# A linear-attention and SwiGLU block: the K feature map by two activations, a transpose moved ahead, and the bursts for M hooked later

## Chip, core and metric

The kernel runs on one NeuronCore of one Trainium2 chip. The metric is device time in microseconds: the median of 6 runs before the change is 715.32 us. The profile is of one further execution, which took 715.18 us.

## What is computed

A layer norm of x (2048 rows of 1024) feeds two branches: linear attention with 32 heads of 32, and a SwiGLU network with 3584 hidden columns.

```python
qkv = (xn @ wqkv)                      # split into q, k, v, 32 heads of 32
phi = lambda t: where(t > 0, t + 1, exp(t)) + 1e-6
pq, pk = phi(q), phi(k)
kv = einsum("bhsd,bhse->bhde", pk, v)
z = einsum("bhsd->bhd", pk)
num = einsum("bhqd,bhde->bhqe", pq, kv)
den = einsum("bhqd,bhd->bhq", pq, z)[..., None] + 1e-6
s = (num / den) @ wo
g = silu((silu(xn @ w_gate) * (xn @ w_up)) @ w_down)
return x + s * g
```

The kernel writes phi as max(t, 0) + (min(exp(t), 1) + 1e-6), which is the same function.

## The kernel before

**Stages.** The 2048 rows are 16 tiles of 128. In the first stage (to about 118 us) every tile is normalised, transposed and multiplied by W_k and W_v, and the products of pk and v are summed over all tiles in three PSUM banks (`a_tile`, L892). Then come two passes of 1024 rows each, in which Q, gate, up, the attention output and the down projection are computed, with the weights loaded for each pass.

**Matrix products with seven steps.** Most products are taken two blocks by two with seven multiplications in place of eight, from sums and differences of blocks that VectorE makes (`combos` for x and W, `x_sums`, `sums` for weights). A `Set` (L580) holds the steps 1 to 7 of one product in PSUM banks: step 1's result is copied to a second bank (`put1`, a ScalarE Identity that reads ps and writes ps), step 5's to SBUF (`put5`), steps 6 and 7 have a VectorE add. A `Joint` (L649) makes step 1 or 5 of two products at once with half-width matmuls (256 columns). The first two tiles are done plainly, by `p_piece` (L879): eight matmuls of 512 columns, four for each half of the depth.

**The start.** x tiles and W_k, W_v blocks of 512 KB come in one after the other on the DMA queue of SyncE (SP). Tiles 0 and 1 are transposed on TensorE (`t_tile`, L802), eight transposes each, whose results ScalarE and VectorE copy to SBUF; the later tiles are transposed by DMA. The source names the pieces in lines 957 to 974: both pieces of tile 0 for K, then tile 1's transposes, then tile 1's pieces.

**The K and Q feature map** (`phi_evac`, L844) takes three instructions for a tile of 128 by 512: a ScalarE Exp out of PSUM (or out of SBUF, for step 7, whose sum VectorE has put there), a VectorE minimum with 1 and addition of 1e-6 (L850, SBUF to SBUF, f16), and a VectorE instruction that takes the maximum of the PSUM tile with 0 and adds (L851). K uses it 32 times, Q 32 times. The Exp results, and those of L850, have rings of two buffers each (L518, L520).

**The bursts for M.** KV, the normalised sum of pk and v, is transposed (`kvt`) and multiplied by W_o into a matrix M (`m_build`, L1053). A burst is 16 matmuls of 32 by 32 with 512 columns; it needs four free PSUM banks at once, ScalarE copies them to SBUF, and four DMAs of SP store them to `m_scratch`, from where they come back as weights about two weight pairs later. There are four bursts. Lines 1708 and 1709 hook them in pass 0: one after step 6 of each of the two Sets of gate pair 0, and the same for up pair 0.

**Who sets the order.** The code only lists the operations with what they read and write. A planner (`Plan`, L35) then places them: it holds a cost for each operation, a due time from TensorE's work (`dl`), a window of six TensorE operations in which the order may be changed (`WINDOW`), and a lead of 12 us for DMA. For ScalarE it holds the function table that is loaded and adds 1.28 us (`TABLE`) for a switch (L228). `tune` (L127) looks for holes on TensorE in its own plan and shifts operations of the other engines. Each engine then runs its list in order, with semaphore waits. So an edit of one cost or one hook can change the order of many instructions. The instructions of all operations are recorded at helper lines: matmuls at L309, transposes at L316, activations at L441, VectorE's tensor-tensor operations at L452, DMAs at L455.

Of the kernel before, what the change touches and what calls it, by code (L numbers as in the profile page):

```python
# [9 lines left out]
ACT = mybir.ActivationFunctionType  # L10
ALU = mybir.AluOpType
F32 = mybir.dt.float32
BF16 = mybir.dt.bfloat16
FP16 = mybir.dt.float16
KB = 1024
# [4 lines left out]
TABLE, DMA_SLACK, HOLD, YIELD = 1.28, 2.0, 0.1, 10  # L20
# [14 lines left out]
class Plan:  # L35
# [143 lines left out]
    def place(self, limit=1e9):  # L179
        ops = self.ops  # L180
        idle = work = 0.0
        for o in ops:
            o.npred = len(o.preds) + len(o.after)
            o.ready = 0.0
        free = {e: 0.0 for e in self.ENGS}
        dma_free = 0.0
        tab = None
        avail = {e: [] for e in self.ENGS}
        pe_next = deque(o for o in ops if o.eng == "pe")
        for o in ops:  # L190
            if o.npred == 0:
                avail[o.eng].append(o)
        order = []
        done = set()
        total = len(ops)
        while len(order) < total:
            best = None
            for e in self.ENGS:
                a = avail[e]
                if not a:  # L200
                    continue
                t = free[e]
                if e == "pe":
                    lim = None
                    n = 0
                    for o in pe_next:
                        if n >= self.window:
                            lim = o.idx
                            break
                        n += 1  # L210
                    cand = [o for o in a if lim is None or o.idx < lim]
                    if not cand:
                        continue
                    rdy = [o for o in cand if o.ready <= t + 0.05]
                    o = min(rdy, key=lambda o: o.idx) if rdy else min(cand, key=lambda o: (o.ready, o.idx))
                else:
                    rdy = [o for o in a if o.ready <= t]
                    soon = [o for o in a if o.ready > t]
                    while rdy:
                        o = min(rdy, key=lambda o: (o.dl - o.boost, o.idx))  # L220
                        q = [q for q in soon if q.ready + HOLD < t + o.busy and q.dl - q.boost + YIELD < o.dl - o.boost] if e != "sp" else ()
                        if not q:
                            break
                        rdy.remove(o)
                    if not rdy:
                        o = min(soon or a, key=lambda o: (o.ready, o.dl))
                s = max(t, o.ready)
                if e == "act" and o.tab is not None and o.tab != tab:  # L228
                    s += TABLE
                if best is None or s < best[0]:  # L230
                    best = (s, e, o)
            s, e, o = best
            if o.tab is not None:
                tab = o.tab
            o.start = s
            was = free[e]
            if o.sem is not None:
                free[e] = s + o.busy
                b = max(s + 1.8, dma_free)
                dma_free = b + o.nbytes / 340e3  # L240
                o.done = dma_free + DMA_SLACK
            else:
                free[e] = s + o.busy
                o.done = s + o.busy + o.lat
            avail[e].remove(o)
            if e == "pe":
                idle += s - was
                work += o.busy
                if work > limit:
                    return idle  # L250
                done.add(o)
                while pe_next and pe_next[0] in done:
                    pe_next.popleft()
            order.append(o)
            for q in o.succs:
                q.npred -= 1
                q.ready = max(q.ready, s + o.busy if q.eng == o.eng and (o.eng == "pe" or o in q.after) else o.done)
                if q.npred == 0:
                    avail[q.eng].append(q)
        self.order = order  # L260
        return idle
# [58 lines left out]
def build_kernel(nc, A_x, A_wqkv, A_wo, B_w_gate, B_w_up, B_w_down, out, WINDOW=6, NWARM=15, NPE=2, LEAD=12.0):  # L320
# [12 lines left out]
    with ExitStack() as es:  # L333
# [27 lines left out]
        TM = Arena("TM", 26 * KB)  # L361
# [66 lines left out]
        def pe_mm(reads, writes, mms):  # L428
            return PL.op("pe", reads, writes, partial(_mm_group, mms), mm_cost(mms))
# [10 lines left out]
        def act(reads, writes, o, i, func, src="ps", **kw):  # L440
            q = PL.op("act", reads, writes, lambda h: h.activation(o, i, func, **kw),  # L441
                      nel(o) / (1000.0 if "bias" in kw or not isinstance(kw.get("scale", 1.0), float) else 1200.0)
                      + (0.055 if src == "ps" else 0.095))
            if func != ACT.Identity:
                PL.table(q, func)
            return q

        def dve(reads, writes, fn, n, rate=0.96):
            return PL.op("dve", reads, writes, fn, n / (rate * 1000.0) + 0.07)

        def tt(reads, writes, o, a, b, op, fast=False):
            return dve(reads, writes, lambda h: h.tensor_tensor(o, a, b, op), nel(o), 1.92 if fast else 0.96)  # L452
# [65 lines left out]
        e_ring = Ring(TM, 20 * KB, 1 * KB, 2)  # L518
        q_ring = Ring(TM, 22 * KB, 1 * KB, 2)
        B_ring = Ring(TM, 24 * KB, 1 * KB, 2)  # L520
        rr_ring = Ring(TM, 20 * KB, 2 * KB, 1)
        x_ring = Ring(W, 32 * KB, 2 * KB, 4)
        xn_ring = Ring(W, 40 * KB, 2 * KB, 2)
# [48 lines left out]
        for n in range(NWARM):  # L572
            b = n % 8
# [267 lines left out]
            return ar.at(j * 8 * KB + k * 4 * KB, 4 * KB, FP16).rearrange("p (q t) -> p q t", t=512)[  # L841
                :, :, m * 128:(m + 1) * 128]

        def phi_evac(src, src_r, out_ap, out_r, kind="ps"):  # L844
            e = e_ring.take()
            ea = e.ap(FP16)
            act([src_r], [e.r], ea, src, ACT.Exp, kind)
            b = B_ring.take()
            ba = b.ap(FP16)
            dve([e.r], [b.r], lambda h: h.tensor_scalar(ba, ea, 1.0, EPS_PHI, ALU.min, ALU.add), 512, 2.6)  # L850
            dve([src_r, b.r], [out_r], lambda h: h.scalar_tensor_tensor(  # L851
                out_ap, src, 0.0, ba, ALU.max, ALU.add), 512)

        kvb = [balloc_part() for _ in range(3)]

# [10 lines left out]
        def k_evac(i, j, ap, r, kind):  # L866
            if i not in pkv:
                pkv[i] = pk_ring.take()
            s = pkv[i].sub(j * 1024, 1024)
            phi_evac(ap, r, s.ap(), s.r, kind)  # L870

        def v_dest(i, j):
            return vext[i % 4][:, 4 * j:4 * j + 4, 0:128]
# [5 lines left out]
        def p_piece(i, w, j):  # L879
            b = balloc(True)  # L880
            n = 2 if (i, w, j) == (0, 0, 1) else 4
            for k0 in range(0, KT, n):
                ap, r = KVV[w]["R%d%d" % (k0 // 4, j)]
                pe_mm([xt_r(i, k0, n), r], [bank_r[b]],
                      [(ps[b][:, :], xt_ap(i, k), ap[:, k % 4, :], k == 0, k == KT - 1) for k in range(k0, k0 + n)])
            if w == 0:
                k_evac(i, j, ps[b][:, :], bank_r[b], "ps")
            else:
                v_evac(i, j, ps[b][:, :], bank_r[b])
            bfree(b)  # L890
# [65 lines left out]
            o.urgent = -4.0  # L956
        ln_tile(1)
        p_piece(0, 0, 1)
        p_piece(0, 0, 0)
        t_tile(1)  # L960
        p_piece(1, 0, 1)
        x_load(4)
        x_load(5)
        p_piece(1, 0, 0)
# [88 lines left out]
        def m_build(g0, c):  # L1053
            bb = [balloc(True) for _ in range(4)]
            mms = []
            for hl in range(4):
                v = slice(32 * hl, 32 * hl + 32)
                for k in range(4):
                    mms.append((ps[bb[hl]][32 * k:32 * k + 32, :], KVT[v, g0 + k, v], wo[c][v, g0 + k, :], True, True))
            pe_mm([KVT_r, wo_r[c]], [bank_r[b] for b in bb], mms).busy = 0.6  # L1060
            s = mst_ring.take()
            for hl, b in enumerate(bb):
                u = s.sub(hl * KB, KB)
                act([bank_r[b]], [u.r], u.ap(FP16), ps[b][:, :], ACT.Identity)
                bfree(b)
            sv = s.ap(FP16).rearrange("p (h n) -> p h n", n=512)
            for k in range(4):
                row = (g0 + k) * 128
                dma([s.r], [named("mscr", c, g0, k)], m_scr[row:row + 128, c * 512:(c + 1) * 512].rearrange(
                    "(h k) n -> k h n", h=4), sv[32 * k:32 * k + 32], dsem("mst%d_%d" % (s.k % 4, k)), 128 * KB)  # L1070
# [631 lines left out]
        for p in range(2):  # L1702
            for k, n in order:
                st = got.pop((k, p, n))
                at = {}
                if (p, k, n) == (0, "q", 0):
                    at = {"5_1": [kv_done], "3_0": [kvt]}
                if p == 0 and (k, n) in (("g", 0), ("u", 0)):
                    at = {"6_0": [build_m], "6_1": [build_m]}
                if (p, k, n) == (0, "g", 1):  # L1710
                    for q in range(4):
                        dma([P.reg(q * 4 * KB, 4 * KB)], [named("xscr", q)], x_scr[q], P.at(q * 4 * KB, 4 * KB, FP16),
# [87 lines left out]
```

## Time and profile before

| | |
|---|---|
| median of 6 runs | 715.32 us (714.68 to 716.15) |
| the profiled execution | 715.18 us |
| its span | 713.4 us |
| TensorE (PE) busy | 704.3 us, 4170 matmuls |
| VectorE (DVE) busy | 640.3 us |
| ScalarE (ACT) busy | 403.3 us |
| ACT_TABLE_LOAD | 8, 1.28 us each |

Times in the profile count from the start of the span. PEld is TensorE's weight load, which overlaps the matmuls. A tile is named by its arena: `ps` is PSUM; `H`, `X`, `P`, `W` and `TM` are parts of SBUF. "out<-in" is what an instruction writes and reads. A bracket at the end of a timeline row gives the idle time of the engine before it, and what ended it. Matmul records overlap, since they are pipelined, so the distance of their starts, not their length, is what one costs; a few records are missing.

### The profile page before, as it was taken

To read this page: it belongs to the slowest core of one execution; us is meant where nothing else is said; L and a number is where in the kernel's file an instruction comes from. 1 tells how busy PE (TensorE), PEld (TensorE's weight loads), DVE (VectorE), ACT (ScalarE), POOL (GpSimd) and SP (SyncE) were. 2 spreads that over 40 slices of the span, in tenths; PEclk is the share of its full clock that TensorE was granted. 3 is DMA by queue.
4 is the path that set the end of the run, shared out by engine and by line. 5 is a ranking of instruction groups with operands and counts; after the bars stand their busy time and mean duration, and the time that the engine had idled before them with its cause. 6 is when DMAs were issued, how large, how long until landed. Compare 5 with 4: busy or idle time off the path is not lost.

```text
span 713.4 us, 11342 instructions
## 1 busy us (share of the span) xinstructions
PE 704.3 (99%) x4170; PEld 388.5 (54%) x4181; DVE 640.3 (90%) x1533; ACT 403.3 (57%) x777; POOL 13.2 (2%) x35
## 2 busy tenths in 40 slices
PE   8999999999999999999999999999999999999998
PEld 3444445455555555556556455555555555565654
DVE  6999988989999999998957999999999999798863
ACT  3667654887679675664122157676886656621212
POOL 2111000000000000000000000000000000000000
PEclk9999999999999999999999999999999999999999
DMA  9625235137364344226485954133715242656663
GB/s 285 157 61 125 52 118 178 60 109 246 120 187 130 126 137 135 86 85 163 146 201 150 270 171 149 60 119 93 203 63 178 89 148 61 174 144 161 142 155 96
DMA packets 140870, 98.64 MB, mean 138 GB/s; under 512 B 34960, under 2 KB 137872, under 8 KB 140816
## 3 DMA queue, kind: packets, MB, share of 16 engines
q1 hardware_dynamic: 140528, 97.74, 48.8%
q8 instruction: 32, 0.52, 0.3%
q10 hardware_dynamic: 288, 0.20, 0.1%
q14 instruction: 22, 0.18, 0.1%
HBM read 77.59 MB, written 12.71 MB: 127 GB/s over the span
## 4 chain that ended last, share of the span: by engine, by line
PE 94%; DVE 3%; DMA 1%; ACT 1%; issue 0%; SPq 0%
PE ps L309 94%; DMA H<-in_A_wqkv_dram 1%; DVE H L851 1%; DVE ps L452 1%; DVE W L452 1%; ACT TM L441 0%; DVE TM L452 0%; DVE H L1037 0%; DVE TM L850 0%; SPq L455 0%; ACT L441 0%; PE ps L316 0%; DVE H L452 0%; SPq L756 0%; DVE X L452 0%
## 5 line engine op out<-in xcount | busy, mean ns | idle before, releaser
L309 PE MATMUL ps<-X,W 128*128 128x512 f16 (+2 forms) x1372 | 288.6, 350 | 0.3 <-DVE ps L452 0.2
L441 ACT ACTIVATE TM<-ps 128x512 f16<-128x512 f32 (+3 forms) x355 | 187.0, 547 | 106.0 <-PE ps L309 101.2
L309 PE MATMUL ps<-H,W 128*128 128x512 f16 (+2 forms) x1090 | 218.0, 351 | 0.4
L452 DVE TENSOR_TENSOR W<-W 128x1024 f16<-128x1024 bf16 (+5 forms) x416 | 186.1, 479 | 5.3 <-PE ps L309 4.5
L309 PEld LDWEIGHTS ps<-X,W 128*128 128x128 f16 (+1 forms) x1372 | 132.4, 98 | 103.9 <-DVE ps L452 1.2
L309 PEld LDWEIGHTS ps<-H,W 128*128 128x128 f16 (+1 forms) x1096 | 105.9, 98 | 95.6 <-DVE ps L452 1.1
L441 ACT ACTIVATE ps<-ps 128x512 f32<-128x512 f32 (+1 forms) x174 | 85.2, 490 | 101.7 <-PE ps L309 99.8
L452 DVE TENSOR_TENSOR ps<-ps,TM 128x256 f32<-128x256 f32 (+1 forms) x250 | 131.0, 526 | 12.7 <-PE ps L309 10.1
L309 PE MATMUL ps<-P,W 128*128 128x256 f16 (+1 forms) x516 | 99.8, 319 | 0.4 <-DVE W L452 0.4
L441 ACT ACTIVATE H<-ps 128x512 f16<-128x512 f32 (+1 forms) x126 | 74.6, 604 | 43.0 <-PE ps L309 43.0
L452 DVE TENSOR_TENSOR H<-H 128x1024 f16<-128x1024 f16 (+5 forms) x126 | 70.8, 577 | 0.8 <-DVE W L789 0.5
L309 PEld LDWEIGHTS ps<-P,W 128*128 128x128 f16 (+1 forms) x516 | 50.3, 98 | 29.7 <-DVE W L452 0.7
L441 ACT ACTIVATE TM<-TM 128x512 f16<-128x512 f32 (+1 forms) x61 | 38.0, 625 | 47.4 <-DVE TM L452 47.1
L309 PE MATMUL ps<-W 128*128 128x256 f16 (+1 forms) x330 | 61.8, 282 | 0.0
L452 DVE TENSOR_TENSOR H<-H,TM 128x512 f16<-128x512 f16 x112 | 45.0, 415 | 8.5 <-ACT H L441 8.4
L452 DVE TENSOR_TENSOR TM<-ps,TM 128x512 f32<-128x512 f32 (+3 forms) x63 | 41.5, 658 | 11.4 <-PE ps L309 10.8
L309 PEld LDWEIGHTS ps<-W 128*128 128x128 f16 (+1 forms) x330 | 31.9, 98 | 31.9 <-DVE ps L452 1.7
L309 PE MATMUL ps<-H,X 128*128 128x512 bf16 (+1 forms) x147 | 35.0, 379 | 1.9 <-DMA H<-in_A_wqkv_dram 1.8
L452 DVE TENSOR_TENSOR H<-ps,TM 128x512 f16<-128x512 f32 (+1 forms) x35 | 24.0, 686 | 3.4 <-PE ps L309 2.6
L309 PE MATMUL ps<-H,P 128*128 128x512 bf16 (+1 forms) x108 | 26.4, 379 | 0.1
L309 PEld LDWEIGHTS ps<-H,X 128*128 128x128 f16 (+1 forms) x150 | 14.1, 98 | 18.9 <-DMA H<-in_A_wqkv_dram 1.9
L452 DVE TENSOR_TENSOR TM<-TM,W 128x512 f16<-128x512 f16 (+1 forms) x39 | 14.1, 363 | 10.5 <-ACT TM L441 10.5
(97 smaller groups left out, 423.0 us busy)
## 6 DMA issues: line engine op xcount, KB each, us to landing
W<-in_B_w_gate_dram SPq DMA_DIRECT2D x14, 1024.0 KB, 5.3
W<-in_B_w_up_dram SPq DMA_DIRECT2D x13, 1024.0 KB, 5.6
W<-in_B_w_down_dram SPq DMA_DIRECT2D x14, 896.0 KB, 6.2
H<-in_A_wqkv_dram SPq DMA_DIRECT2D x8, 512.0 KB, 8.3
H<-r_scratch SPq DMA_DIRECT2D x32, 128.0 KB, 4.0
W<-m_scratch SPq DMA_DIRECT2D x4, 1024.0 KB, 5.4
s_scratch<-TM SPq DMA_DIRECT2D x32, 128.0 KB, 2.3
TM<-in_A_x_dram SPq DMA_DIRECT2D x16, 256.0 KB, 3.7
```

What stands on the lines that cost most here:

```text
L309: last = h.matmul(o, l, r, start=st, stop=sp, skip_group_check=True)
L441: q = PL.op("act", reads, writes, lambda h: h.activation(o, i, func, **kw), nel(o) / (1000.0 if "bias" in kw or not isinstance(kw.get("sca ...
L452: return dve(reads, writes, lambda h: h.tensor_tensor(o, a, b, op), nel(o), 1.92 if fast else 0.96)
L851: dve([src_r, b.r], [out_r], lambda h: h.scalar_tensor_tensor(out_ap, src, 0.0, ba, ALU.max, ALU.add), 512)
```

## The change

The K feature map becomes four instructions: Exp and Relu by ScalarE, both out of the same source, the minimum by VectorE as before, and a VectorE addition of two f16 tiles in SBUF. Relu's results get a ring of two 1 KB buffers. Q keeps its feature map. Tile 1's transposes and its first K piece are named ahead of tile 0's second K piece. The four bursts are hooked after step 6 of the second Set of gate pair 0, of both Sets of up pair 0, and of the second Set of Q pair 1. The planner starts with the Exp table as loaded, lets a table load run while its activation still waits for its operands, takes Relu as needing no table, and counts a burst as 0.42 us of TensorE.

```diff
@@ place
-        tab = None
+        tab = ACT.Exp
...
                 if e == "act" and o.tab is not None and o.tab != tab:
-                    s += TABLE
+                    s = max(t + TABLE, s)
@@ act
-            if func != ACT.Identity:
+            if func not in (ACT.Identity, ACT.Relu):
                 PL.table(q, func)
@@ rings
+        rl_ring = Ring(TM, 18 * KB, 1 * KB, 2)
@@ phi_evac
-        def phi_evac(src, src_r, out_ap, out_r, kind="ps"):
+        def phi_evac(src, src_r, out_ap, out_r, kind="ps", relu=False):
             e = e_ring.take()
             ea = e.ap(FP16)
             act([src_r], [e.r], ea, src, ACT.Exp, kind)
             b = B_ring.take()
             ba = b.ap(FP16)
             dve([e.r], [b.r], lambda h: h.tensor_scalar(ba, ea, 1.0, EPS_PHI, ALU.min, ALU.add), 512, 2.6)
-            dve([src_r, b.r], [out_r], lambda h: h.scalar_tensor_tensor(
-                out_ap, src, 0.0, ba, ALU.max, ALU.add), 512)
+            if not relu:
+                dve([src_r, b.r], [out_r], lambda h: h.scalar_tensor_tensor(
+                    out_ap, src, 0.0, ba, ALU.max, ALU.add), 512)
+                return
+            r = rl_ring.take()
+            act([src_r], [r.r], r.ap(FP16), src, ACT.Relu, kind)
+            tt([r.r, b.r], [out_r], out_ap, r.ap(FP16), ba, ALU.add, True)
@@ k_evac
-            phi_evac(ap, r, s.ap(), s.r, kind)
+            phi_evac(ap, r, s.ap(), s.r, kind, True)
@@ the first pieces
         p_piece(0, 0, 1)
-        p_piece(0, 0, 0)
         t_tile(1)
         p_piece(1, 0, 1)
+        p_piece(0, 0, 0)
@@ m_build
-            pe_mm([KVT_r, wo_r[c]], [bank_r[b] for b in bb], mms).busy = 0.6
+            pe_mm([KVT_r, wo_r[c]], [bank_r[b] for b in bb], mms).busy = 0.42
@@ hooks of pass 0
-                if p == 0 and (k, n) in (("g", 0), ("u", 0)):
-                    at = {"6_0": [build_m], "6_1": [build_m]}
+                if p == 0 and (k, n) in (("g", 0), ("u", 0), ("q", 1)):
+                    at = {"6_1": [build_m]}
+                    if k == "u":
+                        at["6_0"] = [build_m]
```

## The prediction, made before the changed kernel was run

> **What bounds the kernel now.** The page's busy times come first, then who waited for whom on TensorE, then busy time by stage, and last the timeline of the two places where TensorE stood still.
>
> ```profile
> PE 704.3 (99%) x4170; PEld 388.5 (54%) x4181; DVE 640.3 (90%) x1533; ACT 403.3 (57%) x777; POOL 13.2 (2%) x35
> PE ps L309 <- DMA H<-in_A_wqkv_dram: 1.8, 4, 0.8
> PE ps L309 <- DVE TM L452: 1.2, 1, 1.2
> 13.00:27.00 14.00, 13.95 (x76) 6.73 (x77) 13.93 (x38) 8.43 (x13) 3.33 (x4) 1.00 0.92 247
> 50.00:70.00 20.00, 19.90 (x110) 9.82 (x111) 19.10 (x53) 14.61 (x22) 2.85 (x5) 1.00 0.47 106
> 118.00:135.00 17.00, 15.76 (x103) 8.84 (x102) 16.33 (x49) 10.87 (x20) 0.00 (x0) 1.00 0.42 142
> 135.00:153.00 18.00, 17.83 (x151) 8.59 (x152) 14.96 (x43) 16.15 (x34) 0.00 (x0) 1.00 0.23 73
> ```
>
> TensorE is the bound: 704.3 of 713.4 us, with the granted clock at 1.00. The columns of the stage rows are stage, length, PE, PEld, DVE, ACT and POOL. In the K/V stage (27 to 118 us) the waits of that window hold none for a matmul and 1.7 us for weight loads, which the pipeline covers. So all that any edit can win lies in a few holes: the start (before about 13 us), the first burst for M (135 us), and small ones at the other bursts and at the turn from pass 0 to pass 1 (about 0.3 us at 432.9 and 0.4 us at 436.3). What VectorE is spared in the K/V stage is hidden behind TensorE. VectorE is 95% busy there (19.10 of 20) and TensorE doesn't wait; that is the cover of every K edit.
>
> **The start.** Timeline of before, TensorE alone:
>
> ```profile
> 9.67 1.04 PE L309 MATMUL ps<-H,X 128*128 128x512 bf16 x4 [0.30 <-DMA H<-in_A_wqkv_dram]
> 11.18 1.04 PE L309 MATMUL ps<-H,X 128*128 128x512 bf16 x4 [0.47 <-DMA H<-in_A_wqkv_dram]
> 12.05 0.61 PE L316 MATMUL ps<-ident,W 128*128 128x128 f16 x8
> 12.90 12.06 PE L309 MATMUL ps<-H,X 128*128 128x512 bf16 x54 [0.24 <-DMA H<-in_A_wqkv_dram]
> ```
>
> Column one is the start, column two the length. Back to back, eight 512-column matmuls take 1.73 us (130.34 to 132.07 below), 0.216 us each. Four issued at 9.67 are through at 10.53, the next block of W_k lands, and 11.18 starts: a hole of 0.63. Four more end at 12.04, eight transposes take 0.45, and 12.90 follows: a hole of 0.4. In the order of the changed program TensorE goes on from 10.53 with the transposes of tile 1 (its normalised halves were ready at 9.21), which end at about 11.0; then, although the source names tile 1's piece first, the planner puts the first half of tile 0's other K piece (block at 11.18 as before); then tile 1's first half. That half needs ScalarE's copy of the transposes: the Exp of the first piece runs 10.75 to 11.35, the copy about 0.6 after it, 11.9, against 12.04. VectorE's copy ends near 11.6. So from 12.04 TensorE has 0.86 us of work where it had 0.45 of transposes and 0.4 of hole, and the last W_k block is there when it comes: **0.86 us** won. Bounds: nothing, if the copy is late or a later landing takes it back, to 1.0, both holes. The W_v blocks don't move. TensorE's waits for the four W_k blocks end about 1.5 us apart (8.35, 9.67, 11.18, 12.7); carried on at that pace, with two half-size x tiles between, an estimate puts the four W_v blocks at about 15 to 20.1, and TensorE would come for them between 16.4 and 20.7: a margin of about 0.6. I take 0.85.
>
> **The K feature map.** Lines by form (count | busy us, mean ns):
>
> ```profile
> L851 DVE SCALAR_TENSOR_TENSOR TM<-ps,TM 128x512 bf16<-128x512 f32 x25 | 17.1, 683 | 0.2
> L851 DVE SCALAR_TENSOR_TENSOR TM<-TM 128x512 bf16<-128x512 f32 x7 | 4.8, 679 | 0.1
> L452 DVE TENSOR_TENSOR TM<-TM 128x512 bf16<-128x512 f16 x30 | 12.4, 418 | 2.2 <-DMA TM<-TM 1.4 <-DMA TM<-in_A_x_dram 0.7
> L441 ACT ACTIVATE TM<-ps 128x512 f16<-128x512 f32 x180 | 106.8, 598 | 77.6 <-PE ps L309 73.0 <-DMA out_dram<-TM 2.2 <-DVE TM L850 1.2
> L441 ACT ACTIVATE TM<-TM 128x512 f16<-128x512 f32 x59 | 37.2, 632 | 47.3 <-DVE TM L452 47.1 <-DMA s_scratch<-TM 0.2
> ```
>
> Removed: 25 x 0.683 + 7 x 0.679 = 21.8 us of VectorE. Added: 32 x 0.418 = 13.4 of VectorE (the row of an SBUF add of two f16 tiles into bf16, the same form), and 25 x 0.598 + 7 x 0.632 = 19.4 of ScalarE (no Relu is in the trace; an activation of the same shape is the row). VectorE gains 8.4, ScalarE pays 19.4. A pair of tiles is 14 groups of four matmuls and two a_tiles: 14 x 0.86 + 2 x 0.47 = 13.0 us of TensorE. ScalarE had 14.61/20 of that, 9.5; four Relus make it 11.9. VectorE falls from 12.4 to 11.4. Both are under 13.0, so the sum is 0 on TensorE's path. Without cover every us over 13.0 is paid seven times. I put in +0.1 us (bounds -0.1, the few tenths of weight-load waits, and the ScalarE rival's price below).
>
> Here *ScalarE: Activation LUTs* in the Trainium skill (Rules for kernel authors) speaks against the change: relu, max and add belong on VectorE. By that rule 19.4 us of work went to the wrong engine for 8.4 us, and if engine totals were the time, the kernel would lose 11.0. The rows say otherwise: the stage is neither engine's, and ScalarE has 27% of it idle. I go by the rows; the rule's point returns as a rival. The same page (What ACT_TABLE_LOAD costs) gives 2.66 us for a switch of function set, drain included; the trace has 1.28 and the next activation 10 ns later, below. The changed program still has 8 loads, Relu brings none, so switches add 0 by either.
>
> **The first burst for M.**
>
> ```profile
> 130.34 1.89 PE L309 MATMUL ps<-X,W 128*128 128x512 f16 x8
> 132.07 0.38 PE L309 MATMUL ps<-W 128*128 128x256 f16 x2
> 132.51 1.28 ACT L441 ACT_TABLE_LOAD   x1
> 133.37 1.28 DVE L851 SCALAR_TENSOR_TENSOR H<-ps,TM 128x512 bf16<-128x512 f32 x2
> 133.80 1.09 ACT L441 ACTIVATE TM<-ps 128x512 f16<-128x512 f32 x2
> 134.77 0.61 ACT L441 ACTIVATE ps<-ps 128x512 f32<-128x512 f32 x1
> 134.99 0.44 PE L309 MATMUL ps<-H 32*32 32x512 bf16 x16 [1.24 <-DVE TM L452]
> 135.43 2.27 PEld L309 LDWEIGHTS ps<-X,W 128*128 128x128 bf16 x12 [0.30 <-ACT ps L441]
> ```
>
> TensorE's last fed matmul started its pair at 133.37 and is through at 133.6. The burst (16 small matmuls, 0.37 to 0.44) comes at 134.99, 1.4 late, and the matmul after it at 135.43 had to wait for the ps<-ps copy of 134.77, which stood behind a table load and two Silus on ScalarE and behind VectorE's maximum-and-add on its target bank (134.05). So moving the burst alone wins nothing: that copy is late next, at 135.38. What helps is in the order. The edits of the planner (table state at the start, a load that may run while its activation still waits, Relu without a table, 0.42 for a burst) cost nothing by themselves, but they give that order: the copy now stands ahead of the table load, and ahead of that bank's last VectorE instruction there is about 1.0 us less to do (a 1024-column sum of weights, 0.68 busy and 0.6 apart, a 256-column one and a 0.2 us minimum come later). VectorE was full from 118.6 to there, so it frees the bank near 133.0; the copy is there by 133.6, after two other activations; TensorE comes for it at about 133.9, since one pair of 256-column matmuls ahead of it looks 0.3 late (two feature maps precede its VectorE add). Then 12 matmuls, 2.6, and the burst at 136.5; its banks' Silus end at 136.0 (table load to 134.9, two Silus at 0.55 each). Before, the same work, burst included, was through at 138.04; after, 136.96: **1.1 us** won; bounds 0 and 1.4.
>
> The other bursts: their prices stay (about 0.46 each). Extra waits of 0.1 near 142.5 and 0.2 after the last one (152.36) fall in the stage where ScalarE is 90% busy (16.15 of 18); one burst's four copies leave it: -0.2. New: the fourth burst, in the second Q pair, waits for VectorE, since its banks held Q results that an Exp (0.6), a minimum (0.2) and a maximum-and-add (0.68) must clear: 1.75 with hand-overs, against 2.6 us of matmuls put in between. VectorE's queue in 153 to 185 is 97% busy and a table load is near; +0.3 (bounds 0, +1.4). Behind it on the DMA queue stand its four stores to m_scratch, at about 0.47 each, and weight loads; those loads were issued well ahead before, and the second half of W_o now goes out one weight load later, for a burst some 10 us later: 0. At the turn of the passes one feature map moves ahead of a sum and others behind: 0 (bounds -0.4, +0.4). After it only bank numbers differ.
>
> **Sum.** -0.85 - 1.1 - 0.2 + 0.3 + 0.1 = -1.75. The profiled execution took 715.18 (span 713.4, 1.8 around it), so 713.4; on the median of 715.32, 713.6. I say 713.5.
>
> **Rivals.** (1) *ScalarE becomes what the K/V stage waits for*; slower. Its work per pair is 11.9 of 13.0, in a fixed order, with waits of its own: in 27 to 118 us it waited 6.1 us in 6 turns for VectorE's sums, about 1.0 per pair. If those stay whole and the rest doesn't fit, the overrun is paid by all seven pairs. For: 11.9 + 1.0 leaves 0.1. Against: VectorE at 12.4 of 13.0 made nobody wait, and activations overlap by 0.05 to 0.1 (two in 1.09 where one takes 0.6). From 0.45 us per pair on it decides (3.2 us); at 0.6, 715.3 - 1.8 + 4.2 = 717.7. (2) *Part of the gain doesn't come*: the copy is as late as before, or the start's gain is taken back by landings, or the fourth burst pays in full. One of these leaves 0.4 to 0.9: 714.6. (3) *The edits do nothing*, since only hidden work moves: 715.3. Against it: two holes that can be measured are reordered. I fold it into (2).
>
> **How the numbers follow.** Likeliest 0.60: 712.4 to 713.9. Rival 2 with 3: 0.24, 713.9 to 716.0. Rival 1: 0.16, from 716.0. A measurement of this kernel tells about 0.2%, 1.4 us, from no change, so these are also faster, same and slower. The lower end 712.4 is both holes and no new wait; the upper, 716.4, takes in rival 2 and the near part of rival 1.
>
> **What would show it.** Right: tile 1's transposes near 10.6 us and no hole at 12.9; VectorE's wait ahead of the first burst gone, the ps<-ps copy ahead of the table load; in 50 to 70 us ScalarE near 18 and VectorE near 17.5 of 20 with TensorE as full as before; 32 Relus of about 0.6. Wrong: TensorE waiting for ScalarE's banks at 27 to 118 us, or over a microsecond at the fourth burst or at the turn of the passes.

## The result

The changed kernel takes 713.24 us (median of 15 runs, 711.75 to 715.02) where the kernel before, run beside it 34 times, takes 715.4: a ratio of 0.9968, with a 95% interval of 0.9961 to 0.9975. Measured a second time, beside other kernels, it was 713.57 against 715.48, 0.9975 (0.9965 to 0.9985). So it is 1.9 to 2.2 us faster; 713.5 was predicted. The profiled execution took 712.54 us, its span is 710.6.

The page of the changed kernel, and its list of who TensorE waits for (us in total, times, longest):

```profile
PE 704.3 (99%) x4170; PEld 388.2 (55%) x4181; DVE 634.0 (89%) x1533; ACT 416.8 (59%) x809; POOL 14.1 (2%) x35
```

```profile
PE ps L309 <- DVE TM L571: 1.0, 1, 1.0
PE ps L309 <- DVE ps L452: 0.7, 2, 0.3
PE ps L316 <- DVE TM L452: 0.6, 1, 0.6
PE ps L316 <- DVE W L790: 0.2, 1, 0.2
```

TensorE's work is the same to a tenth of a microsecond. Three rows of before are gone: the waits for W_k blocks (1.8), the one for VectorE's sum (1.2), which stood ahead of the first burst, and one of 0.4 for a sum of weights at the turn of the passes. The row of 0.7 was 0.2 before; its two turns are the pair of 256-column matmuls ahead of the first burst (0.30, in the timeline of the burst below) and one at the turn of the passes (0.35). Stage by stage (stage, length, then PE, PEld, DVE, ACT and POOL):

```profile
27.00:50.00 23.00, 22.89 (x118) 10.93 (x119) 21.87 (x60) 20.19 (x33) 2.51 (x4) 1.00 0.47 100
50.00:70.00 20.00, 19.89 (x110) 9.82 (x110) 18.57 (x53) 16.54 (x28) 2.61 (x5) 1.00 0.49 115
70.00:118.00 48.00, 47.74 (x271) 23.99 (x275) 34.52 (x84) 31.25 (x57) 1.14 (x2) 1.00 0.29 85
118.00:135.00 17.00, 16.70 (x112) 8.74 (x109) 16.98 (x48) 11.72 (x21) 0.00 (x0) 1.00 0.53 170
```

TensorE is as full in 27 to 118 us as before. VectorE there has 0.4 to 0.5 us less to do in each of the first two rows, and most of what it is spared shows in the third (40.89 before). ScalarE's added work comes mostly early: 14.61 became 20.19 of 23, 14.61 became 16.54 of 20, 27.20 became 31.25 of 48. In 118 to 135 us TensorE went from 15.76 to 16.70.

The instruction groups that the feature map touches, by form (count | busy us, mean ns | idle before):

```profile
L441 ACT ACTIVATE TM<-ps 128x512 f16<-128x512 f32 x205 | 119.5, 600 | 74.6 <-PE ps L309 71.6 <-DVE TM L851 1.3 <-DVE TM L452 1.1
...
L441 ACT ACTIVATE TM<-TM 128x512 f16<-128x512 f32 x66 | 41.5, 634 | 46.0 <-DVE TM L452 45.7
...
L452 DVE TENSOR_TENSOR TM<-TM 128x512 bf16<-128x512 f16 x62 | 25.7, 418 | 4.0 <-DMA TM<-TM 1.6 <-ACT TM L441 1.3 <-DMA TM<-in_A_x_dram 0.8
```

25 and 7 more activations, 32 more additions of 0.418 us; K's 32 maximum-and-adds are gone.

The start, TensorE alone:

```profile
7.53 1.94 PE L309 MATMUL ps<-H,X 128*128 128x512 bf16 x8
9.31 0.61 PE L316 MATMUL ps<-ident,W 128*128 128x128 f16 x8
9.94 12.26 PE L309 MATMUL ps<-H,X 128*128 128x512 bf16 x54
```

No row has a bracket: after 7.53 TensorE waits for no block. But the first W_k block landed at 6.90 us here and at 8.22 in the profile of before, and no edit touches that. How much of the earlier start is the change's was left to the experiments.

The first burst, TensorE and ScalarE (rows of two timelines):

```profile
129.42 0.60 ACT L441 ACTIVATE ps<-ps 128x512 f32<-128x512 f32 x1
130.01 0.39 PE L309 MATMUL ps<-W 128*128 128x256 f16 x2 [0.30 <-DVE ps L452]
130.24 4.48 PE L309 MATMUL ps<-X,W 128*128 128x512 f16 x20
130.98 0.58 ACT L441 ACTIVATE ps<-ps 128x512 f32<-128x512 f32 x1
131.58 1.28 ACT L441 ACT_TABLE_LOAD   x1
134.65 0.43 PE L309 MATMUL ps<-H 32*32 32x512 bf16 x16
```

The copy ps<-ps stands ahead of the table load, the burst comes without a wait, and so do the other three. What the prediction had not seen is at 188 us (SPq is SP's DMA queue; "landed" is not shown in this view, the load of 178.99 landed at 188.51):

```profile
178.48 0.46 SPq L455 DMA_DIRECT2D x_scratch<-P  x1
178.99 0.45 SPq L455 DMA_DIRECT2D W<-in_B_w_up_dram  x1
179.48 1.34 SPq L455 DMA_DIRECT2D x_scratch<-P  x1
...
188.54 1.30 DVE L452 TENSOR_TENSOR W<-W 128x256 f16<-128x256 bf16 x4 [0.64 <-DMA W<-in_B_w_up_dram]
```

A load of 1 MB of weights took 9.52 us from issue to landing, where it took 5.65 before; VectorE waited for it, and TensorE stood 0.1 and 0.3 us at 190.2 and 190.8 for sums behind it.

### The profile page after: what moved, and what is told of

Same layout as the page of the kernel before. It is cut to its first block, busy times and chain, and to the rows that moved or that the text cites. A ratio compares the mean times of both kernels' runs of the same rounds, so it can differ in the third digit from the quotient of the medians.

```text
span 710.6 us, 11395 instructions
## 1 busy us (share of the span) xinstructions
PE 704.3 (99%) x4170; PEld 388.2 (55%) x4181; DVE 634.0 (89%) x1533; ACT 416.8 (59%) x809; POOL 14.1 (2%) x35
## 4 chain that ended last, share of the span: by engine, by line
PE 94%; DVE 3%; DMA 2%; ACT 0%; issue 0%; SPq 0%
PE ps L309 94%; DMA W<-in_B_w_up_dram 1%; DVE ps L452 1%; DVE H L853 1%; DVE W L452 0%; DMA W<-in_A_x_dram 0%; ACT TM L441 0%; DVE H L1043 0%; SPq L455 0%; DVE TM L851 0%; PE ps L316 0%; DVE TM L452 0%; DVE stats L773 0%; DVE stats L774 0%; DVE W L790 0%
## 5 line engine op out<-in xcount | busy, mean ns | idle before, releaser
L441 ACT ACTIVATE TM<-ps 128x512 f16<-128x512 f32 (+3 forms) x380 | 199.6, 552 | 102.2 <-PE ps L309 99.0
L441 ACT ACTIVATE TM<-TM 128x512 f16<-128x512 f32 (+1 forms) x68 | 42.4, 628 | 46.2 <-DVE TM L452 45.7
L452 DVE TENSOR_TENSOR TM<-TM 128x512 bf16<-128x512 f16 (+2 forms) x73 | 29.5, 411 | 6.6 <-ACT TM L441 3.9
```

## The experiments

All medians in us, each ratio against the runs of the kernel before that were made beside it.

| kernel | median | before beside it | ratio | 95% interval |
|---|---|---|---|---|
| changed, first time | 713.24 | 715.40 | 0.9968 | 0.9961 to 0.9975 |
| changed, second time | 713.57 | 715.48 | 0.9975 | 0.9965 to 0.9985 |
| changed, start order undone | 714.24 | 715.64 | 0.9981 | 0.9974 to 0.9987 |
| changed, Relu undone | 714.74 | 715.64 | 0.9989 | 0.9980 to 0.9998 |
| changed, hooks undone | 714.38 | 715.64 | 0.9984 | 0.9977 to 0.9990 |
| changed, table edits undone | 714.78 | 715.64 | 0.9988 | 0.9980 to 0.9997 |
| before, start order alone | 715.76 | 715.48 | 1.0004 | 0.9996 to 1.0013 |
| before, hooks alone | 714.60 | 715.48 | 0.9990 | 0.9982 to 0.9999 |
| before, Relu alone | 715.43 | 715.68 | 0.9996 | 0.9987 to 1.0005 |
| changed, every Relu twice | 714.06 | 715.68 | 0.9977 | 0.9968 to 0.9986 |
| changed, stores of x earlier | 712.99 | 715.68 | 0.9964 | 0.9952 to 0.9977 |
| the same, and x read back later | 712.61; 714.77 | 715.48; 715.68 | 0.9967; 0.9983 | 0.9956 to 0.9979; 0.9971 to 0.9995 |

Single medians can't carry this alone: the intervals are 1 to 2 us wide, and the kernel of the last row, measured twice, has medians 2.2 us apart. Each profile, though, shows its own holes to a hundredth. So I read four sums from the starts of consecutive matmuls in every profile (a matmul of 512 columns is due 0.216 us after the one before it, so what is above that is a hole; the 0.18 by which a matmul follows a block of transposes late is the same everywhere and left out). The profiles of before and of the changed kernel, first time, hold 4170 matmul records and the others 4181; in each of those two, between 10 and 115 us, there are eleven holes of one matmul's length (0.21 to 0.25; one of them is part of the hole before 12.90 in before), a series that the others don't have. These are taken as missing records and left out too.

The sums are:

- start: when the first K matmul starts, plus all holes after it until 45 us, minus the landing of the first W_k block;
- bursts: all holes from 128 to 168 us;
- 190: holes there;
- turn: the two holes at 430 to 437 us, where the passes change.

| profile | first W_k landed | start | bursts | 190 | turn |
|---|---|---|---|---|---|
| before | 8.22 | 1.37 | 3.26 | 0 | 0.88 |
| before, Relu alone | 7.61 | 1.31 | 3.26 | 0 | 0.88 |
| before, hooks alone | 7.21 | 1.53 | 2.07 | 0.44 | 0.89 |
| before, start order alone | 7.95 | 2.19 | 3.27 | 0 | 0.89 |
| changed, start order undone | 6.75 | 1.59 | 2.09 | 0.70 | 0.63 |
| changed, table edits undone | 8.09 | 1.43 | 2.09 | 0 | 0.89 |
| changed, Relu undone | 7.67 | 1.93 | 2.09 | 0.53 | 0.63 |
| changed, hooks undone | 7.62 | 0.68 | 3.27 | 0 | 0.63 |
| changed | 6.90 | 0.63 | 2.09 | 0.40 | 0.62 |
| changed, second time | 6.25 | 1.26 | 2.08 | 0 | 0.63 |
| changed, every Relu twice | 7.92 | 0.75 | 2.09 | 0.48 | 0.63 |
| changed, stores of x earlier | 6.99 | 0.81 | 2.09 | 0 | 0.62 |

Bursts and turn fall into two values each. In the second profile of the changed kernel the first block came so early that tile 0's own transposes, which end near 7.5 us, were the limit; its 1.26 isn't a wait for blocks and is left out of what follows. In three more profiles the transposes were the limit of the first matmul, which came 0.63 to 0.81 us after the landing: changed, stores of x earlier, and start order undone. Where TensorE waits for the block, it comes 0.13 or 0.14 behind it (0.30 with the hooks alone). So the hole ahead of the third W_k block, which doesn't depend on this, is read beside the start sums.

### The start order undone

```diff
         p_piece(0, 0, 1)
+        p_piece(0, 0, 0)
         t_tile(1)
         p_piece(1, 0, 1)
-        p_piece(0, 0, 0)
```

> The changed kernel with the source order of the start put back (both halves of tile 0's K piece ahead of tile 1's transposes); everything else as changed. The prediction's step: the two holes come back, TensorE waits some 0.4 us ahead of the matmuls at 12.9 us and about 0.6 ahead of the W_k block before, and the median is 0.85 above the changed kernel's 713.24: 714.1. Rival (the earlier landings made the start, not the order): the changed kernel's profile had its W_k blocks 1.25 us sooner than the profile of before; if that luck, and not the reordering, filled the holes, this kernel has no holes either when its blocks land soon, and its median is 713.2 to 713.5.

714.24, as the prediction's step has it. Its first block landed earlier than the changed kernel's (6.75), and the hole ahead of the third block is there all the same; so it isn't luck. TensorE's timeline:

```profile
9.97 1.04 PE L309 MATMUL ps<-H,X 128*128 128x512 bf16 x4 [0.48 <-DMA H<-in_A_wqkv_dram]
10.84 0.61 PE L316 MATMUL ps<-ident,W 128*128 128x128 f16 x8
11.46 1.90 PE L309 MATMUL ps<-H,X 128*128 128x512 bf16 x8
```

There is no hole behind the transposes, though, in this kernel or in the two with the hooks or the Relu alone: the next matmul is 0.17 to 0.18 late, as it is behind every block of transposes, a hand-over. The 0.4 that the prediction read at 12.90 in the profile of before is that hand-over and one of the eleven missing records: the block landed at 12.63, the weight load for its first matmul is recorded at 12.67, and one matmul of 0.22 us fits between that and 12.90.

### The Relu undone

```diff
-            phi_evac(ap, r, s.ap(), s.r, kind, True)
+            phi_evac(ap, r, s.ap(), s.r, kind)
```

> The changed kernel with K's feature map as before (VectorE's maximum-and-add from PSUM, no Relu on ScalarE); start, bursts and planner as changed. The prediction's step: the K edit lies beside TensorE's work, so 713.1 to 713.3 (0 to 0.1 below the changed kernel), no wait in 27 to 118 us, the first burst without a wait of over 0.5. Rival (VectorE's spared 8 us is what frees the bank of the first burst in time): the wait of about 1.2 us for VectorE ahead of the first burst is back, near 714.3.

714.74: 1.2 to 1.5 above the changed kernel's two medians. Both theories missed the place. The first burst is as good as in the changed kernel, so the rival's bank is not it; but the start is worse than before's. TensorE and VectorE there:

```profile
16.52 0.70 DVE L773 BATCH_NORM_STATS2 stats<-W 128x6 f32<-128x512 bf16 x1
17.13 0.68 DVE L774 BATCH_NORM_STATS2 stats<-W 128x6 f32<-128x512 bf16 x1
17.72 0.67 DVE L853 SCALAR_TENSOR_TENSOR TM<-ps,TM 128x512 bf16<-128x512 f32 x1
...
18.45 1.90 PE L309 MATMUL ps<-H,X 128*128 128x512 bf16 x8 [0.70 <-DVE TM L853]
```

TensorE arrives earlier, thanks to the new order, and asks for K's bank again before VectorE, busy with sums of blocks that have just landed and with the statistics of the next tiles, has read it. With the Relu the bank's last reader is ScalarE, which has room (5.70 of the 7.00 us from 13 to 20 busy in the changed kernel). The hole is 0.87 us, and small ones follow at 34 to 43 us (0.25, 0.09, 0.10): together more than the start order wins.

### The hooks undone

```diff
-                if p == 0 and (k, n) in (("g", 0), ("u", 0), ("q", 1)):
-                    at = {"6_1": [build_m]}
-                    if k == "u":
-                        at["6_0"] = [build_m]
+                if p == 0 and (k, n) in (("g", 0), ("u", 0)):
+                    at = {"6_0": [build_m], "6_1": [build_m]}
```

with the burst's price back at 0.6.

> The changed kernel with the four bursts for M where they were (two in each of the first gate and up pair) and priced 0.6 as before; Relu, start and planner as changed. The prediction's step (moving the burst alone wins nothing; the planner's edits give the order that does): 713.0 to 713.4. Rival (the place of the burst gives the order): in this program the copy of the bank's sums stands behind ScalarE's table load again, TensorE waits about 1 us or more ahead of the burst near 134 us, and the time is 714.3.

714.38, the rival's value. ScalarE's and TensorE's rows:

```profile
131.08 1.28 ACT L441 ACT_TABLE_LOAD   x1
132.38 1.09 ACT L441 ACTIVATE TM<-ps 128x512 f16<-128x512 f32 x2
133.35 0.60 ACT L441 ACTIVATE ps<-ps 128x512 f32<-128x512 f32 x1
...
133.56 0.44 PE L309 MATMUL ps<-H 32*32 32x512 bf16 x16 [1.24 <-DVE TM L452]
```

The copy is behind the table load again although all edits of the planner's table are in, and the hole of 1.40 us between starts is back to the hundredth.

### The planner's table edits undone

```diff
-        tab = ACT.Exp
+        tab = None
...
-                    s = max(t + TABLE, s)
+                    s += TABLE
```

> The changed kernel with the planner's two edits of the table load taken back (no table at the start, a load added after the activation's inputs are there); hooks, burst price, Relu and start as changed. The prediction's step (these edits give the order at the first burst): the gain of 1.1 goes, 714.3. Rival (the hooks give it): the copy stands ahead of the table load without the edits too, and the time is 713.2 to 713.5, the difference made by small moves elsewhere.

714.78, near the prediction's value, and for another reason. The first burst is untouched; ScalarE's rows there:

```profile
132.91 0.58 ACT L441 ACTIVATE ps<-ps 128x512 f32<-128x512 f32 x1
133.51 1.28 ACT L441 ACT_TABLE_LOAD   x1
```

What is lost is the start and the turn. In the changed kernel's list for TensorE, eight matmuls of tile 1's K piece stand between the four of tile 0 that need the third W_k block and the four that need the fourth; without these edits the planner lists tile 0's two fours in a row, and the hole is only put off by one block:

```profile
10.53 0.61 PE L316 MATMUL ps<-ident,W 128*128 128x128 f16 x8
11.16 1.04 PE L309 MATMUL ps<-H,X 128*128 128x512 bf16 x4
12.65 7.73 PE L309 MATMUL ps<-H,X 128*128 128x512 bf16 x35 [0.45 <-DMA H<-in_A_wqkv_dram]
```

The block landed at 12.60. Which of the two edits does it wasn't tried.

By their distance from before (1.40, 0.90, 1.26 and 0.86, against 2.16), the four parts undone one by one lose 0.8 to 1.3 us each, 4.2 in all, twice the gain. Either the start is one gain that three of the parts share, or everything gained less in these runs. So the changed kernel comes again, and parts alone.

### The changed kernel again

> The changed kernel once more, beside the three others of this call and their runs of before. If the four kernels with one part undone lay 0.8 to 1.3 below before because each part is worth that much only together with the others, the changed kernel is again about 2.2 below before here (ratio 0.9964 to 0.9974). If those runs were merely taken under conditions in which everything gains less, it is only about 1.2 below (0.998).

713.57, 0.9975. It is about 1.9 below before, but the interval (1.1 to 2.5 us) doesn't exclude 1.2. That the parts belong together is therefore read from the holes, and from the parts alone.

### The start order alone

In the kernel before:

```diff
         p_piece(0, 0, 1)
-        p_piece(0, 0, 0)
         t_tile(1)
         p_piece(1, 0, 1)
+        p_piece(0, 0, 0)
```

> The kernel before with the source order of the start alone changed (tile 1's transposes and first half ahead of tile 0's other K half). The prediction's step: 0.85 below before, whatever the other parts. Rival (the start needs the other two): without the planner's table state TensorE's order has both halves of tile 0's piece in a row, so the hole of 0.6 us moves to the fourth W_k block; without the Relu, K's banks are released by VectorE, which can be held up at a sum of W_v blocks (0.87 us at 18.4 us in the run without the Relu). Then 0 to 0.3 below before.

No gain: 1.0004. Both conditions that it lacks show in TensorE's rows:

```profile
12.48 11.71 PE L309 MATMUL ps<-H,X 128*128 128x512 bf16 x52 [0.46 <-DMA H<-in_A_wqkv_dram]
...
29.89 1.04 PE L309 MATMUL ps<-H,X 128*128 128x512 bf16 x4 [0.44 <-ACT ps L441]
```

The hole has moved to the fourth block (0.62 between starts), and three more come at 17, 19 and 30 us (0.16, 0.12, 0.60). By the start sums (2.19 against 1.31 to 1.59) it should lose 0.6 to 0.9 us; the measured interval, -0.3 to +0.9 us, holds that.

### The hooks alone

In the kernel before, with the burst's price at 0.42:

```diff
-                if p == 0 and (k, n) in (("g", 0), ("u", 0)):
-                    at = {"6_0": [build_m], "6_1": [build_m]}
+                if p == 0 and (k, n) in (("g", 0), ("u", 0), ("q", 1)):
+                    at = {"6_1": [build_m]}
+                    if k == "u":
+                        at["6_0"] = [build_m]
```

> The kernel before with only the four bursts for M hooked later and priced 0.42. The prediction's step (moving a burst alone wins nothing at the first, the others give 0.2 and the fourth takes 0.3): 0.0 to 0.2 from before. Rival (the place of the burst is what puts the bank's copy ahead of the table load): TensorE's wait ahead of the first burst (1.40 us) goes, 0.5 remain at the pair of 256-column matmuls before it; with the other bursts 0.9 to 1.3 below before.

714.60, the near end of the rival's range. The first burst is as in the changed kernel, without Relu, start order or table edits (the burst's price goes with the hooks here, and which of the two does it wasn't tried):

```profile
131.25 0.39 PE L309 MATMUL ps<-W 128*128 128x256 f16 x2 [0.30 <-DVE ps L452]
131.48 4.48 PE L309 MATMUL ps<-X,W 128*128 128x512 f16 x20
135.89 0.43 PE L309 MATMUL ps<-H 32*32 32x512 bf16 x16
```

The wait at 190 us is there too (0.44), so it comes with the hooks. 3.26 - 2.07 - 0.44 = 0.75 won by the holes, 0.88 by the medians.

### The Relu alone

In the kernel before, with the new `phi_evac` and its ring:

```diff
-            phi_evac(ap, r, s.ap(), s.r, kind)
+            phi_evac(ap, r, s.ap(), s.r, kind, True)
...
-            if func != ACT.Identity:
+            if func not in (ACT.Identity, ACT.Relu):
```

> The kernel before with only K's feature map changed (Relu and Exp on ScalarE, VectorE's add from SBUF; Relu counted as needing no table). The prediction's step: 0 to 0.1 above before, since the work moved lies beside TensorE's; the two holes of the start (0.6 and 0.2 to 0.4) and the 1.40 us ahead of the first burst stay. Rival (freeing K's banks by ScalarE is worth something by itself, as the run without it lost 0.7 to 1.3): 0.7 or more below before.

0.9996 (0.9987 to 1.0005), no difference that can be told. By itself moving K's work gives TensorE nothing, as the prediction's step has it; the rival falls. It counts only with the new start.

### Every Relu twice

```diff
             act([src_r], [r.r], r.ap(FP16), src, ACT.Relu, kind)
+            act([src_r], [r.r], r.ap(FP16), src, ACT.Relu, kind)
```

> The changed kernel with every Relu of K issued twice (the second writes the same values again): 32 more activations of 0.58 us, 18.6 of ScalarE. The changed kernel's ScalarE has 20.2 of 23 us at 27 to 50 and 16.5 of 20 at 50 to 70, or 11.1 per pair of tiles of 13.0; four more make it 13.4. If the stage ends where ScalarE's work per pair passes 13.0 (the prediction's rival 1), TensorE waits for it in 27 to 118 us and seven pairs at 0.4 cost 2.8: 716.0 to 716.6; with ScalarE's own waits of about 1.0 per pair kept whole, up to 723. If there is other slack, the time stays at 713.2 to 713.9.

714.06, 0.9977, with nearly the interval of the changed kernel's second measurement (0.9975). The median is 0.2 above the range for other slack, 0.5 and 0.8 above the changed kernel's two, and about 2 us under the least that rival 1 would give; the one hole in the stage is 0.09. Its stage rows:

```profile
27.00:50.00 23.00, 23.00 (x119) 10.78 (x118) 21.85 (x60) 21.77 (x39) 4.46 (x5) 1.00 0.41 92
50.00:70.00 20.00, 20.00 (x112) 9.82 (x111) 18.59 (x53) 19.97 (x34) 2.68 (x4) 1.00 0.52 118
70.00:118.00 48.00, 48.00 (x276) 23.82 (x275) 34.35 (x82) 39.24 (x74) 1.21 (x2) 1.00 0.29 81
```

ScalarE is full for 20 us (19.97 of 20), and TensorE is full beside it. What is late there is caught up after 70 us, where 39.24 of 48 are taken. So the price of rival 1, the overrun paid by all seven pairs, is wrong, by this run: the work of ScalarE isn't the same for each pair, and an engine that is full for a while holds nobody up while its results aren't due. That ScalarE bounds the stage at some larger load isn't excluded, but the changed kernel is more than 14.7 us of ScalarE away from it (431.5 busy here, 416.8 in the changed kernel).

### The late load

```diff
-                if (p, k, n) == (0, "g", 1):
+                if (p, k, n) == (0, "u", 0):
                     for q in range(4):
                         dma([P.reg(q * 4 * KB, 4 * KB)], [named("xscr", q)], x_scr[q], P.at(q * 4 * KB, 4 * KB, FP16),
                             dsem("xp%d" % q), 512 * KB, after=PL.lastpe)
```

> The changed kernel with only the stores of x to the scratch issued one and a half pairs earlier, so that the W_up load near 179 us has four stores for M ahead of it and none of x around it. If the stores of x made it late (8.4 to 9.8 us with the hooks moved, 5.65 in before), it lands in 5.5 to 6.5 us, the wait of 0.1 to 0.7 us near 190 us is gone, and the time is 0.2 to 0.5 below the changed kernel. Rival: the wait moves to another load; no gain.

The load takes 5.31 us and nobody waits:

```profile
176.74 1.76 SPq L455 DMA_DIRECT2D m_scratch<-H  x4
179.22 0.40 SPq L455 DMA_DIRECT2D W<-in_B_w_up_dram  x1
192.01 0.39 SPq L455 DMA_DIRECT2D W<-in_B_w_gate_dram  x1
```

With the hooks moved and the stores of x where they were, it took 8.4 to 9.8 us, and TensorE's holes near 190 us were between 0 and 0.70 in seven profiles. With the stores moved it took 5.31, and 5.29 and 5.38 in the two profiles of the second version below, although the four stores for M still stand ahead of it. So the stores of x around it make it late, and the late hooks bring it there. The time of 712.99 is 0.25 and 0.6 below the changed kernel's two medians; the intervals of the ratios overlap, so a gain is what the trace says, and not what the times can tell.

A second version also tried to get the second pass's W_q load out from behind the reading back of x:

```diff
                 dma([named("xscr", q)], [P.reg(q * 4 * KB, 4 * KB)], P.at(q * 4 * KB, 4 * KB, FP16), x_scr[q],
-                    dsem("xl%d" % q), 512 * KB)
+                    dsem("xl%d" % q), 512 * KB).urgent = -3.0
```

> The changed kernel with two moves of transfers: the stores of x to the scratch are issued one and a half pairs earlier, so that the W_up load near 179 us no longer stands among them, and in the turn of the passes the reading back of x is due 3 us later, so that the second pass's W_q load stands ahead of it. If late loads make the waits at 190 us (0.4 in the changed kernel's profile, up to 0.7 in others) and 409 us (0.14 to 1.03), both go: 0.5 to 1.2 below the changed kernel of the same call. Rival: what is read back later is late in turn, and the time is the same or up to 1 us above.

712.61 from five runs, 0.9967; it looked like the best. It was run once more:

> The kernel with both transfers moved once more, beside the one with only the stores moved, since its interval overlapped the changed kernel's. If both moves count, it lies 0.5 to 1.2 below the changed kernel's 713.2 to 713.6 again and 0.2 to 0.7 below the other; if only the stores count, the two are equal.

714.77 from twelve runs, 0.9983. This profile shows what the rival said: VectorE doesn't wait for W_q any more, but 0.85 us for the x that is now read later, TensorE's hole at 409 us is 0.98 all the same, and a load behind them is late in turn:

```profile
435.67 0.39 PE L309 MATMUL ps<-P,X 128*128 128x256 f16 x2 [0.43 <-DMA X<-in_B_w_up_dram]
...
436.59 0.39 PE L309 MATMUL ps<-P,X 128*128 128x256 f16 x2 [0.21 <-DVE X L452]
```

In this profile the new order of the transfers decided only which one is late. That the move gains anything isn't shown.

## Why the prediction was right, and where it was not

- **The bound and the stage.** Right. TensorE stayed at 704.3, no wait in 27 to 118 us, and the Relu alone makes 0.9996. The rule of the Trainium skill that was weighed (*ScalarE: Activation LUTs*, Rules for kernel authors: relu and add belong on VectorE), priced as lost engine time, would have cost 11 us; it cost nothing that can be told. Two sizes were off. ScalarE's busy time rose by 13.5 (403.3 to 416.8) and not 19.4: 32 activations add 0.6 each only if none overlaps its neighbour, and here two in a row take 1.09. ScalarE in 50 to 70 us is 16.5, not near 18, and VectorE 18.6, not near 17.5.
- **The start, -0.85.** The mechanism and nearly the size hold for the whole change. The hole ahead of the third W_k block, 0.59 to 0.64 in the four profiles with the old order at the start, is in none with the whole new start: -0.6. The start sums give about -0.73: 1.31 to 1.59 (mean 1.45) in those four, and 0.63 to 0.81 (mean 0.72) in four with the whole new start (the changed kernel, with the hooks undone, with every Relu twice, with the stores of x earlier), but three of these eight hold the late transposes. Where the first matmul waits for the block, they are 1.31 and 1.37 against 0.68 and 0.75, -0.63. The mis-sized term is the second hole, of which 0.22 was a missing record and the rest a hand-over that stays. What failed is the K edit's "the sum is 0 on TensorE's path" and the planner's edits that "cost nothing by themselves", each taken alone: the start order needs both. Without the Relu a hole of 0.87 at 18.45 takes it back, without the table edits one of 0.61 at 12.65; alone it gains nothing.
- **The first burst, -1.1.** The size is nearly right and its reason is wrong. The failed step is "moving the burst alone wins nothing ... the edits of the planner ... give that order". The runs show the opposite: hooks alone give the order and the gain, all the other edits without them give neither. 1.40 + 0.37 became 0.46 + 0.38 (the pair and the burst's own 0.38): -0.93. The pair of 256-column matmuls is 0.46 late, predicted 0.3; "the burst at 136.5", without a wait, is right, at 134.65 on the earlier clock.
- **The other bursts, -0.2, and the fourth, +0.3.** The first came, and a little more (0.12 + 0.23 gone). The fourth doesn't wait: 160.35 follows its matmul as the others do, 0 in place of 0.3, and a hole of 0.10 comes at 165.2. All bursts: 2.09 - 3.26 = -1.17, predicted -1.0.
- **"Behind it on the DMA queue ... weight loads: 0."** This failed. The W_up load behind those stores and among the stores of x took 9.52 us from issue to landing, 5.65 before, and TensorE's holes behind it average 0.36 over the seven profiles that have the late hooks and the old stores (0.40, 0, 0.70, 0, 0.53, 0.44, 0.48): +0.36.
- **The turn, 0 within 0.4.** It is -0.26 (0.88 to 0.62), and goes with the table edits: 0.88 to 0.89 in all five profiles without them, 0.62 to 0.63 in all others but the kernel that reads x back later.

The sum as measured is -0.73 - 1.17 + 0.36 - 0.26 = -1.8, or -1.7 with the start at -0.63; the medians say -2.2 and -1.9, the prediction -1.75. The total was right while the parts were credited to the wrong edits, and the closeness is partly luck: +0.36 at the late load and -0.26 at the turn, neither of them foreseen, nearly cancel. The spans of the profiled pair differ by 2.8, and 1.3 of that is the first block that landed earlier.

Rival 1 fell in the changed kernel and in the run with twice the Relus. Of rival 2 no named way came; the part of the gain that was lost went to the wait at 190 us, which it didn't name. Open is what makes TensorE's hole at 409 us vary from 0 to 1.03 between these profiles: in eight of the eleven that have it VectorE had waited for the W_q load before it, and the hole is about as long as that wait (with the Relu alone 1.02 and 1.1, with the hooks alone 0.37 and 0.4, in the changed kernel 0.14 and 0.2); in three it had not.

## What to carry to other kernels

Undoing each part and doing each part alone give different answers when parts share one gain: here three edits are needed for one gain at the start, and the leave-one-out losses summed to about twice the whole gain. Read an engine's slack from when its results are due, not from its load per iteration, and ask of a bank not only what work is spared but which engine reads it last. Where a new order puts a weight load between two large stores, look at when it lands, even where it was issued in good time.

## What was not expected of the hardware

- The first W_k block, issued the same way in every kernel here, landed between 6.25 and 8.22 us in the twelve profiles of the table; the blocks behind it keep a distance of about 1.5 us. This moves the whole execution, so a single pair of profiles can't price an edit of the start.
- A 1 MB load took 5.3 to 5.4 us with no store of x near it and 8.4 to 9.8 us between two such stores of 512 KB, one issued 0.5 us ahead of it and one 0.5 us behind.
- 32 activations of 0.6 us added only 13.5 us to ScalarE's busy time: neighbours overlap (two in a row take 1.09).
